# Splitting an accumulator's evacuation between ScalarE and VectorE, with the rounds of a fused convolution and MLP rearranged and its weights laid out in pairs

## The chip, the cores and the metric

One Trainium2 chip, one core. The metric is the device time of one execution in microseconds (us). A time is a median of several runs. A ratio is the mean time of one kernel's runs over that of the other kernel's runs of the same timing rounds (not the *rounds* of the kernel, which are explained below), so it is not quite the ratio of the medians quoted beside it. The interval is at 95%.

TensorE does the matmuls, into the memory called PSUM; ScalarE (ACT) and VectorE (DVE) read what it leaves there; GpSimd (POOL) works here on a buffer `E` in SBUF, the core's working memory; SyncE (SP), ACT and POOL start DMA transfers.

## The reference

```
w   = softmax(weight, over the 7 taps)            # 8 heads x 7
a   = causal depthwise conv of x[8, 4096, 192] with w (24 channels share a head)
h   = a.reshape(32768, 192) @ w_in                # 192 -> 2048
g   = where(h > 0, h, exp(min(h, 0)) - 1)         # ELU
out = g @ w_out                                   # 2048 -> 192, float32
```

## The kernel before

The tokens go through in 32 superblocks of 1024. Each superblock has 16 *up-projections*, one for each chunk of 128 of the 2048 features (six matmuls of 64x128 by 64x512 into one of three buffers of H in PSUM). ACT, POOL and DVE turn a buffer of H into `gT`. The *down-projection* is cut into *rounds* of two matmuls that add to `ops`, two PSUM banks, and are strewn between the up-projections. 64 rounds make one finished accumulator of 256 + 256 tokens; I call that stretch (8 up-projections, 64 rounds, one conv in two parts) a *half*. In the middle of each half stands one conv for a later superblock, which takes a turn of the three H buffers too.

How many rounds stand in which gap is set by tables:

```python
LAG = -3
GAPS = ((10,), (10,), (6,), (6,), (10,), (5, 6), (11,))
WCOLS = ((0, 256), (256, 640), (640, 1280), (1280, 2048))   # w_in is loaded in four pieces
EARLY_CONV = {3: (1, 0), 6: (1, 1), 9: (2, 0)}   # first convs, by up-projection
```

ELU of one tile, for each up-projection n and each u in (0, 1). `exp` is on ACT, the clamp on POOL, the rest on DVE:

```python
a.activation(E[:, n % NE, u, :], H[:, k, GS*u : GS*(u+1)], ACT.Exp)               # exp(h)
g.tensor_scalar(out=E[...], in0=E[...], 1.0, 0.0, op0=ALU.min, op1=ALU.max)       # min(exp(h), 1)
v.scalar_tensor_tensor(out=gT[...], in0=E[...], scalar=1.0, in1=H[...],
                       op0=ALU.subtract, op1=ALU.max)                              # max(E - 1, h)
```

An up-projection that takes a buffer of H waits until DVE is through with what was in it:

```python
def wait_slot(k):
    was = prior[k]
    ...
    if was[0] == "h":
        W(s_tt, 2 * was[1] + 2)
    else:
        conv_read(W, was[1])
```

With nine turns of three buffers in a half, the same places meet in every half. I number the up-projections behind the conv u1 to u8 (u8 is the last before the next conv). Then u4 takes the buffer of u1, u5 that of u2, and so on to u8, which takes u5's; the conv takes that of u6, u1 that of u7, and u2 that of u8; only u3 takes the conv's.

The finished accumulator is evacuated by ACT alone, in one copy of 2 x 384 columns, and the first round of the next half waits for it:

```python
def evac(key):
    W(s_swap, mm2_done[key])
    W(s_out[b], 32 * (n_half // 2))
    ...
    a.activation(osb[:, b].rearrange("p g k d -> p g (k d)"), ops[:, :, 0 : 2 * D], ACT.Copy).then_inc(s_oev)
```

## Time and profile before

| | before |
|---|---|
| time, median (range) | 747.87 us (747.39 to 748.05) |
| span of the profile | 746.5 us |
| busy: PE, DVE, ACT, POOL | 98, 85, 87, 89% |
| one half, in the steady part | 11.27 us |
| the part of it that is matmul work | 10.84 us |
| start of up-projection 25 | 49.12 us |

Two lines of the page of before: the busy time of each engine (us, share of the span, instructions), and the chain that ended last by engine.

```profile
PE 731.6 (98%) x11866; PEld 505.4 (68%) x11866; DVE 638.0 (85%) x1042; ACT 646.8 (87%) x1224; POOL 664.5 (89%) x1108
...
PE 93%; DVE 2%; POOL 2%; DMA 1%; ACT 1%; issue 0%
```

TensorE is the engine on the chain. A busy share of 98% says little about how well it is used, because overlapping matmuls count as busy: the 3072 of the up-projection take 378 ns each, 1161 us one after another, and their group is busy for 409.2 us. A better measure is the time from the start of one group of matmuls to the start of the next. Here is the timeline of before, TensorE's rows of one half with the rows of ACT and POOL that matter. Columns: start, duration (both us), engine, line, operation, written from read, shapes, how many merged, and in brackets how long the engine stood idle before and what ended it.

```profile
222.36 1.07 PE L770 MATMUL ops<-w_out,gT 64*128 64x192 f16 x22
...
223.27 1.46 PE L735 MATMUL H<-att,w_in 64*128 64x512 bf16 x12
223.54 0.82 ACT L474 ACTIVATE osb<-ops 128x768 f32<-128x768 f32 x1
...
224.23 3.10 ACT L515 ACTIVATE E<-H 128x512 f32<-128x512 f32 x6
...
224.56 0.99 PE L770 MATMUL ops<-w_out,gT 64*128 64x192 f16 x20
224.93 7.11 POOL L414 TENSOR_SCALAR E<-E 128x512 f32<-128x512 f32 x12 [0.47 <-ACT E L515]
...
225.39 0.81 PE L735 MATMUL H<-att,w_in 64*128 64x512 bf16 x6
...
226.03 0.99 PE L770 MATMUL ops<-w_out,gT 64*128 64x192 f16 x20
...
226.91 0.82 PE L735 MATMUL H<-att,w_in 64*128 64x512 bf16 x6
```

Six up-projection matmuls take 0.645 us (twelve take 224.56 - 223.27 = 1.29), a round takes about 0.0825 us (ten: 225.39 - 224.56 = 0.83), a part of the conv 0.20 us. So 8 x 0.645 + 64 x 0.0825 + 2 x 0.20 = 10.84 us is the work of a half. At 226.03 ten rounds take 0.88 us: the up-projection behind them is 0.05 us late. The 0.82 us copy on ACT stands in front of exponentials, and POOL is idle for 0.47 us before its run of clamps.

The same waits summed by who waited for whom (from 44 to 725 us of before; total us, times, longest):

```profile
POOL E L414 <- ACT E L515: 53.9, 159, 1.0
PEld ops L770 <- ACT osb L474: 11.2, 61, 0.2
PEld H L735 <- DVE gT L579: 8.5, 37, 0.4
```

PEld is the weight load. It runs ahead of the matmuls, so an idle weight loader is not yet an idle TensorE (one case in the timeline of after, below: 0.43 us of the one, 0.12 us of the other).

### The profile page before, as it was taken

What the parts mean: (1) busy time and instruction counts of PE and PEld (TensorE: products, weight loads), DVE (VectorE), ACT (ScalarE), POOL (GpSimd) and SP (SyncE); (2) the same over time, 40 slices, a digit from 0 to 9 for tenths busy, and PEclk for the clock granted to TensorE, in tenths of its full rate; (3) what the DMA queues carried; (4) which work ended last, traced back from release to release, by engine and by line L of the source; (5) the groups of instructions that cost most, each with busy time, mean ns of one, the idle gap of its engine ahead of it and who ended that gap; (6) DMA issues with size and microseconds to landing.
All of it is one profiled execution on the core that took longest, in us unless ns stands there. A gap on an engine that the chain in (4) does not pass through costs nothing.

```text
span 746.5 us, 28038 instructions
## 1 busy us (share of the span) xinstructions
PE 731.6 (98%) x11866; PEld 505.4 (68%) x11866; DVE 638.0 (85%) x1042; ACT 646.8 (87%) x1224; POOL 664.5 (89%) x1108
## 2 busy tenths in 40 slices
PE   6899999999999999999999999999999999999997
PEld 3466667666766676666766766766766766766666
DVE  5789889889889888898898898898898898888894
ACT  4888988988988988888989989989989989889883
POOL 8799999999899999899999899999999899898893
PEclk9999999999999999999999999999999999999999
DMA  9544435535435535345535345635345444244212
GB/s 168 93 76 91 62 70 93 94 61 92 63 68 94 93 60 95 57 74 95 82 71 94 46 84 94 77 77 70 64 91 94 67 87 81 53 89 81 46 44 66
DMA packets 132881, 58.93 MB, mean 79 GB/s; under 512 B 98068, under 2 KB 132372, under 8 KB 132756
## 3 DMA queue, kind: packets, MB, share of 16 engines
q0 software_dynamic: 44160, 17.28, 22.9%
q1 hardware_dynamic: 88308, 39.37, 21.9%
q8 instruction: 93, 1.52, 0.9%
q10 hardware_dynamic: 288, 0.49, 0.2%
q14 instruction: 32, 0.26, 0.1%
HBM read 35.61 MB, written 25.17 MB: 81 GB/s over the span
## 4 chain that ended last, share of the span: by engine, by line
PE 93%; DVE 2%; POOL 2%; DMA 1%; ACT 1%; issue 0%
PE H L735 45%; PE ops L770 44%; PE H L703 3%; DVE gT L579 2%; DMA xg<-in_x_dram 1%; ACT E L515 1%; POOL E L414 1%; PE H L770 1%; POOL w_in L369 1%; ACT csb L485 0%; POOL xg L364 0%; PE ops L703 0%; ACT osb L474 0%; PE ops L615 0%; POOL sel L384 0%
## 5 line engine op out<-in xcount | busy, mean ns | idle before, releaser
L579 DVE SCALAR_TENSOR_TENSOR gT<-E,H 128x512 f16<-128x512 f32 x1024 | 632.5, 681 | 90.9 <-POOL E L414 84.4
L414 POOL TENSOR_SCALAR E<-E 128x512 f32<-128x512 f32 x1024 | 603.9, 615 | 69.5 <-ACT E L515 62.1
L515 ACT ACTIVATE E<-H 128x512 f32<-128x512 f32 x1024 | 546.2, 608 | 73.5 <-PE H L735 64.8
L770 PE MATMUL ops<-w_out,gT 64*128 64x192 f16 x8064 | 426.4, 243 | 0.3
L770 PEld LDWEIGHTS ops<-w_out,gT 64*128 64x128 f16 x8064 | 346.9, 94 | 110.5 <-ACT osb L474 11.4
L735 PE MATMUL H<-att,w_in 64*128 64x512 bf16 x3072 | 409.2, 378 | 2.9 <-DVE gT L579 1.7
L735 PEld LDWEIGHTS H<-att,w_in 64*128 64x128 bf16 x3072 | 130.9, 94 | 111.7 <-DVE gT L579 12.8
L485 ACT ACTIVATE csb<-H 128x480 bf16<-128x480 f32 x118 | 60.9, 568 | 7.4 <-PE H L703 0.4
L474 ACT ACTIVATE osb<-ops 128x768 f32<-128x768 f32 x63 | 52.0, 826 | 6.2 <-PE ops L770 6.2
L364 POOL DMA_DIRECT2D xg<-in_x_dram x62 | 55.7, 899 | 0.1
L703 PE MATMUL H<-xg,Tm 64*128 64x240 bf16 x472 | 44.0, 263 | 0.1
L703 PEld LDWEIGHTS H<-xg,Tm 64*128 64x128 bf16 x472 | 21.2, 94 | 0.8 <-DVE gT L579 0.3
L485 ACT ACTIVATE csb<-ops 128x480 bf16<-128x480 f32 x6 | 3.5, 588 | 3.2 <-PE ops L703 3.2
L770 PE MATMUL H<-w_out,gT 64*128 64x192 f16 x128 | 5.9, 243 | 0.0
L703 PE MATMUL ops<-xg,Tm 64*128 64x240 bf16 x24 | 2.7, 306 | 3.3 <-DMA xg<-in_x_dram 3.1
L590 DVE COPY osb<-H 128x192 f32<-128x192 f32 x1 | 0.4, 358 | 6.3 <-PE H L770 6.3
L770 PEld LDWEIGHTS H<-w_out,gT 64*128 64x128 f16 x128 | 5.3, 94 | 0.0
L369 POOL DMA_DIRECT2D w_in<-in_moe_w_in_dram x7 | 4.6, 663 | 0.3 <-DMA wh<-in_weight_dram 0.3
L610 PE MATMUL ops<-zw 128*128 128x512 bf16 x9 | 3.6, 577 | 1.2 <-DVE zw L527 1.2
L615 PE MATMUL ops<-zw 64*128 64x512 bf16 x12 | 2.4, 381 | 2.3 <-ACT csb L485 2.3
L703 PEld LDWEIGHTS ops<-xg,Tm 64*128 64x128 bf16 x24 | 0.9, 97 | 5.2 <-issue 3.5
L615 PEld LDWEIGHTS ops<-zw 64*128 64x128 bf16 x12 | 0.6, 93 | 4.2 <-ACT csb L485 3.9
(49 smaller groups left out, 26.3 us busy)
## 6 DMA issues: line engine op xcount, KB each, us to landing
out_dram<-osb SPq DMA_DIRECT2D x126, 192.0 KB, 4.1
xg<-in_x_dram POOLq DMA_DIRECT2D x61, 240.0 KB, 5.6
w_out<-in_moe_w_out_dram POOLq DMA_DIRECT2D x1, 768.0 KB, 16.1
att<-csb SPq DMA_TRANSPOSE x31, 6.4
w_in<-in_moe_w_in_dram POOLq DMA_DIRECT2D x2, 240.0 KB, 9.0
xf<-in_x_dram ACTq DMA_DIRECT2D x1, 384.0 KB, 3.2
xf<-in_x_dram SPq DMA_DIRECT2D x1, 384.0 KB, 3.6
w_in<-in_moe_w_in_dram POOLq DMA_DIRECT2D x2, 144.0 KB, 4.2
```

Of the source, the lines that this page charges most:

```text
L364: g.dma_start(xg[:, b, v0 : v0 + whole, :], src).then_inc(s_x[b][part - 1], 16)
L369: g.dma_start(w_in[HP * r : HP * (r + 1), :, c0:c1], moe_w_in.rearrange("(p j) f -> p j f", j=3)[:, :, c0:c1],).then_inc(s_w[k], 16)
L414: g.tensor_scalar(out=E[:, n % NE, u, :], in0=E[:, n % NE, u, :], scalar1=1.0, scalar2=0.0, op0=ALU.min, op1=ALU.max,).then_inc(s_clp)
L474: a.activation(osb[:, b, :, :, :].rearrange("p g k d -> p g (k d)"), ops[:, :, 0 : 2 * D], ACT.Copy,).then_inc(s_oev)
L485: return a.activation(csb[:, s % 2, :].rearrange("p (j v h i) -> p h j v i", j=3, v=2 * WPG, h=HEADS)[:, h0 : h0 + HB], conv_bank(m)[:, b, ...
L515: a.activation(E[:, n % NE, u, :], H[:, k, GS * u : GS * (u + 1)], ACT.Exp).then_inc(s_exp)
L579: v.scalar_tensor_tensor(out=gT[:, s % NG3, q, u, :], in0=E[:, n % NE, u, :], scalar=1.0, in1=H[:, slot_of_pair[n] % 3, GS * u : GS * (u + ...
L610: pe.matmul(ops[:, 0, :], zw[:, 0:P], zw[:], start=True, stop=True)
L615: pe.matmul(ops[:, r, :], zw[HP * r : HP * (r + 1), 0:P], zw[HP * r : HP * (r + 1), :], start=True, stop=True, tile_position=(HP * r, 0),)
L703: ins = pe.matmul(to[:, b, n1 * hh : n1 * (hh + 1)], Tm[HP * rt : HP * (rt + 1), h, :], xg[HP * rt : HP * (rt + 1), s % NXB, :, :].rearran ...
L735: ins = pe.matmul(H[:, k % 3, GS * r : GS * (r + 1)], w_in[HP * r : HP * (r + 1), j, FC * q : FC * (q + 1)], att[HP * r : HP * (r + 1), s ...
L770: ins = pe.matmul(acc[:, g, d0 : d0 + D], gT[HP * rt : HP * (rt + 1), t % NG3, q, g, t0 : t0 + P], w_out[HP * rt : HP * (rt + 1), q, :], s ...
```

## The change

The intent is to relieve ACT: the copy is split, ACT takes bank 0 and DVE bank 1. The rounds are laid out anew (rounds 0, 1, 16, 7, 7, 7, 6, and 7 + 3 + 10 around the parts of the conv). The first convs come later. Features are paired: a partition takes two neighbouring rows of w_out, which makes runs of 1536 and not 768 bytes in that load, and w_in is read at stride 2 to match. The w_out load is also issued last.

```diff
-LAG = -3
-GAPS = ((10,), (10,), (6,), (6,), (10,), (5, 6), (11,))
-WCOLS = ((0, 256), (256, 640), (640, 1280), (1280, 2048))
+LAG = -5
+GAPS = ((), (1,), (16,), (7,), (7,), (7,), (6,), (7, 3, 10))
+WCOLS = ((0, 256), (256, 768), (768, 1280), (1280, 2048))
-EARLY_CONV = {3: (1, 0), 6: (1, 1), 9: (2, 0)}
+EARLY_CONV = {6: (1, 0), 8: (1, 1), 10: (2, 0)}
 ... (the order of the program follows GAPS)
             load_x(2, 1)
+            load_x(2, 2)
             g.dma_start(
-                w_out[:, :, :], moe_w_out.rearrange("(q p) d -> p q d", p=FC)
+                w_out.rearrange("p (q r) d -> p q (r d)", r=2), moe_w_out.rearrange("(q p r) d -> p q (r d)", p=FC, r=2)
             ).then_inc(s_w[4], 16)
-            load_x(2, 2)
 ... (ACT)
-                a.activation(
-                    osb[:, b, :, :, :].rearrange("p g k d -> p g (k d)"),
-                    ops[:, :, 0 : 2 * D],
-                    ACT.Copy,
-                ).then_inc(s_oev)
+                out_ready(W, key)
+                a.activation(*out_pieces(key, 0), ACT.Copy).then_inc(s_oev)
 ... (DVE now walks the program's order)
+            for item in order:
+                if item[0] == "o":
+                    for key in item[2]:
+                        out_ready(W, key)
+                        v.tensor_copy(*out_pieces(key, 1)).then_inc(s_od)
 ... (TensorE)
-                                w_in[HP * r : HP * (r + 1), j, FC * q : FC * (q + 1)],
+                                w_in[HP * r : HP * (r + 1), j,
+                                    2 * FC * (q // 2) + q % 2 : 2 * FC * (q // 2 + 1) : 2],
                                 W(s_oev, place[key])
+                                W(s_od, place[key])
```

More of the change, by code (lines that the diff above doesn't have):

```diff
@@ L24 @@
 BN = HB * CPH * 2 * WPG
-GAP_SPLIT = 4
 TAP = 6
@@ L32 @@
 NG3 = 2
-LAG = -3
-GAPS = ((10,), (10,), (6,), (6,), (10,), (5, 6), (11,))
-WCOLS = ((0, 256), (256, 640), (640, 1280), (1280, 2048))
-Q_PART = (0,) * 2 + (1,) * 3 + (2,) * 5 + (3,) * 6
+LAG = -5
+GAPS = ((), (1,), (16,), (7,), (7,), (7,), (6,), (7, 3, 10))
+WCOLS = ((0, 256), (256, 768), (768, 1280), (1280, 2048))
+Q_PART = (0,) * 2 + (1,) * 4 + (2,) * 4 + (3,) * 6
 WARM = (9, 1)
 CONV_AT = ((2, 1, 1), (10, 2, 0))
-EARLY_CONV = {3: (1, 0), 6: (1, 1), 9: (2, 0)}
+EARLY_CONV = {6: (1, 0), 8: (1, 1), 10: (2, 0)}
 FREE_CONV = 3
@@ L84, in bass_lightweight_conv__then__act_elu_kernel, with conv_at @@
     order = []
-    def conv_at(s, g, gap=None):
+    def conv_at(s, g, between=None):
         m = 2 * s + g - 2
@@ L90, in conv_at @@
         order.append(("c", m, 0))
-        between = []
-        if gap:
-            between, gap[:] = gap[:GAP_SPLIT], gap[GAP_SPLIT:]
         if between:
@@ L139, in bass_lightweight_conv__then__act_elu_kernel @@
         gaps = list(rounds_at.get(n, ()))
-        if len(gaps) == 2:
-            order.append(("o", gaps.pop(0)))
-        if n in EARLY_CONV:
-            conv_at(*EARLY_CONV[n])
-        if s:
-            for at, ahead, g in CONV_AT:
-                if at == i and s + ahead < NS:
-                    conv_at(s + ahead, g, gaps[0] if gaps else None)
-        if gaps and gaps[0]:
-            order.append(("o", gaps[0]))
+        convs = [EARLY_CONV[n]] if n in EARLY_CONV else []
+        convs += [
+            (s + ahead, g)
+            for at, ahead, g in CONV_AT
+            if at == i and s + ahead < NS and 2 * (s + ahead) + g - 2 >= FREE_CONV
+        ]
+        if convs and len(gaps) == 3:
+            order.append(("o", gaps[0]))
+            conv_at(*convs[0], gaps[1])
+            order.append(("o", gaps[2]))
+            continue
+        for conv in convs:
+            conv_at(*conv)
+        for gap in gaps:
+            order.append(("o", gap))
     last_slot = [take_slot(None) for _ in range(2)]
@@ L326, in out_group, with out_ready, out_pieces @@
             eng.dma_start(dst, osb[:, b, g, :, :]).then_inc(s_out[b], 16)
+        def out_ready(W, key):
+            t, half, kb = key
+            n_half = 2 * t + half
+            W(s_swap, mm2_done[key])
+            W(s_out[n_half % 2], 32 * (n_half // 2))
+        def out_pieces(key, g):
+            t, half, kb = key
+            b = (2 * t + half) % 2
+            if (t, half) == (last, 1):
+                return osb[:, b, g, kb, :], H[:, last_slot[kb] % 3, GS * g : GS * g + D]
+            return (
+                osb[:, b, g, :, :].rearrange("p k d -> p (k d)"),
+                ops[:, g, 0 : 2 * D],
+            )
         def turn_att(eng, s):
@@ L454, in evac @@
             def evac(key):
-                t, half, kb = key
-                n_half = 2 * t + half
-                W(s_swap, mm2_done[key])
-                b = n_half % 2
-                W(s_out[b], 32 * (n_half // 2))
-                if (t, half) == (last, 1):
-                    if kb == 0:
-                        a.activation(
-                            osb[:, b, :, 0, :],
-                            H[:, last_slot[0] % 3, :].rearrange("p (g t) -> p g t", g=2)[:, :, 0:D],
-                            ACT.Copy,
-                        ).then_inc(s_oev)
-                    else:
-                        a.activation(
-                            osb[:, b, 0, 1, :], H[:, last_slot[1] % 3, 0:D], ACT.Copy
-                        ).then_inc(s_oev)
-                        W(s_od, 1)
-                        out_group(a, t, half, 1, 1)
-                    return
-                a.activation(
-                    osb[:, b, :, :, :].rearrange("p g k d -> p g (k d)"),
-                    ops[:, :, 0 : 2 * D],
-                    ACT.Copy,
-                ).then_inc(s_oev)
+                out_ready(W, key)
+                a.activation(*out_pieces(key, 0), ACT.Copy).then_inc(s_oev)
+                if key == (last, 1, 1):
+                    W(s_od, place[key] + 1)
+                    out_group(a, last, 1, 1, 1)
             late = []
@@ L572, in _vector @@
             v.tensor_copy(Tm[:], Tr[:, :, ::-1]).then_inc(s_tm)
-            for n in range(NP):
-                s, q = divmod(n, NQ)
-                if s >= NG3:
-                    W(s_swap, mm2_done[s - NG3, 1, 0])
-                for u in range(2):
-                    W(s_clp, 2 * n + u + 1)
-                    v.scalar_tensor_tensor(
-                        out=gT[:, s % NG3, q, u, :],
-                        in0=E[:, n % NE, u, :],
-                        scalar=1.0,
-                        in1=H[:, slot_of_pair[n] % 3, GS * u : GS * (u + 1)],
-                        op0=ALU.subtract,
-                        op1=ALU.max,
-                    ).then_inc(s_tt)
-            b = (2 * NS - 1) % 2
-            W(s_swap, mm2_done[last, 1, 1])
-            W(s_out[b], 32 * (NS - 1))
-            v.tensor_copy(
-                osb[:, b, 1, 1, :], H[:, last_slot[1] % 3, GS : GS + D]
-            ).then_inc(s_od)
+            for item in order:
[3 more added lines that the diff above has]
+                        v.tensor_copy(*out_pieces(key, 1)).then_inc(s_od)
+                elif item[0] == "h":
+                    n = item[1]
+                    s, q = divmod(n, NQ)
+                    if s >= NG3:
+                        W(s_swap, mm2_done[s - NG3, 1, 0])
+                    for u in range(2):
+                        W(s_clp, 2 * n + u + 1)
+                        v.scalar_tensor_tensor(
+                            out=gT[:, s % NG3, q, u, :],
+                            in0=E[:, n % NE, u, :],
+                            scalar=1.0,
+                            in1=H[:, slot_of_pair[n] % 3, GS * u : GS * (u + 1)],
+                            op0=ALU.subtract,
+                            op1=ALU.max,
+                        ).then_inc(s_tt)
         @block.tensor
@@ L736, in _tensor @@
                                 H[:, k % 3, GS * r : GS * (r + 1)],
-                                w_in[HP * r : HP * (r + 1), j, FC * q : FC * (q + 1)],
+                                w_in[
+                                    HP * r : HP * (r + 1),
+                                    j,
+                                    2 * FC * (q // 2) + q % 2 : 2 * FC * (q // 2 + 1) : 2,
+                                ],
                                 att[HP * r : HP * (r + 1), s % 2, j, 0:GS],
@@ L814, in _sync @@
                         t, half, kb = key
-                        W(s_oev, place[key] + 1)
-                        if (t, half) != (last, 1):
-                            for g in range(2):
+                        for g in range(2):
+                            W((s_oev, s_od)[g], place[key] + 1)
+                            if (t, half) != (last, 1):
                                 out_group(sy, t, half, g)
-                        elif kb == 0:
-                            for g in range(2):
-                                out_group(sy, t, half, g, 0)
-                        else:
-                            out_group(sy, t, half, 0, 1)
+                            elif (g, kb) != (1, 1):
+                                out_group(sy, t, half, g, kb)
             for b in range(2):
```

## The prediction

> **What bounds it now.** TensorE. The page gives PE 98% busy, and the chain of waits that ended last is 93% PE, nearly all of it the two matmul groups (up-projection into H 45%, down-projection into ops 44%). Reading start-to-start times in the timeline, six up-projection matmuls take 0.645 us, a down-projection round of two takes 0.0825 us, and half a conv takes 0.20 us. A half-superblock (8 up-projections, 64 rounds, two conv halves) therefore needs 5.16 + 5.28 + 0.40 = 10.84 us. From 44 to 725 us it really takes about 11.21 us, so only 0.37 us of each half (22 us in all) is not matmul work. Most of this, about 18 us, is TensorE waiting before an up-projection for one of the three H buffers to be freed by DVE; about 3 us is the hand-over inside the conv. The evacuation of ops (0.83 us on ACT, 63 times) is not a direct wait: two up-projections (1.29 us) hide it. It delays the next exponentials, though: POOL then idles 0.47 us per half (in the timeline, waiting for ACT) and runs its clamps back to back (0.59 us each), so the next H buffers come free late. ACT, POOL and DVE are 87, 89 and 85% busy.
>
> **What the change does.**
> - ACT's 768-column copy becomes 384 on ACT and 384 on DVE in parallel. My estimates from the 0.83 us (768 columns) and 0.36 us (192 on DVE): about 0.43 us on ACT, 0.5 us on DVE. ACT loses 25 us in all, DVE gains about 30 us and goes to 89-90%.
> - Rounds are rearranged with the same counts: a long gap of 16 after three near-adjacent up-projections, then even gaps of 6-7, and 20 around the conv. Total TensorE work is unchanged. Walking one half with the trace's latency (2.8 us from the end of an up-projection to DVE freeing its buffer) I get waits of 0.1-0.2 us before the second up-projection after the conv, almost none in the even gaps, and one more bank hand-over at the conv (0.05 us). Estimate: 11.09 us per half instead of 11.21, about 7 us over 61 halves.
> - Early convs move from pairs 3, 6, 9 to 6, 8, 10. This removes the 3.05 us wait for the conv input (landing at 18.2 us), but pairs from 10 on then meet the last w_in copy (issued 20.1, 6.3 us to land). Net about 2 us.
> - w_out's load has half as many pieces, twice as long[...]; w_out is not waited for in this trace, so I count nothing.
> - w_in weights are read at stride 2 bf16.[...] Each load shows 94 ns[...].
>
> **Predicted:** 739 us, range 730 to 747. Faster by over 2%: 0.18; within 2%: 0.79; slower by over 2%: 0.03.
>
> **What would show it.** Right: ACT's osb copies near 0.43 us with DVE copies near 0.5 us; up-projection weight loads still 94 ns; the wait of up-projections for DVE halves; POOL's idle before the clamps falls; period per half near 11.1 us; the first down-projection starts some 3 us earlier; no wait on the conv input at 15-18 us.
>
> **What would make it wrong.** DVE's copy sits in order in front of gate work: if it delays freeing buffers, or the round after two up-projections waits for DVE's copy, the gain vanishes (745-750).[...] If the waits vanish altogether and the start gains over 4 us, it is near 728.

The sum: 747.87 us of before, less about 7 for the steady part and about 2 for the start, is 739.

## The result, and the profile after

| | before | after |
|---|---|---|
| time, median (range) | 747.87 us (747.39 to 748.05) | 743.3 us (742.13 to 744.1) |
| ratio to before | | 0.9939 (0.9921 to 0.9956) |
| span of the profile | 746.5 us | 741.6 us |
| one half, from up-projection 57 to 489 (54 halves) | 11.27 us | 11.20 us |
| start of up-projection 25 | 49.12 us | 47.92 us |

Of the 4.9 us between the two spans, 1.2 us are there at up-projection 25; another 3.9 us come by up-projection 489, evenly but for 0.4 us that before loses once between 201 and 217; the rest of the program gives 0.2 us back. The 1.2 us are one profile against one, and that of after starts late: its first up-projection begins at 12.53 us and that of before at 10.76 (why, is told under the table of the runs). Counted from there, 38.36 us to up-projection 25 became 35.39.

The page of after, the same two lines:

```profile
PE 730.1 (98%) x11866; PEld 502.6 (68%) x11866; DVE 657.3 (89%) x1106; ACT 636.4 (86%) x1224; POOL 663.7 (89%) x1108
...
PE 94%; DMA 3%; POOL 1%; ACT 0%; DVE 0%; issue 0%
```

ACT went from 646.8 to 636.4 us and DVE from 638.0 to 657.3. The groups of after that do the evacuation, and the weight loads of the up-projection (busy us, mean ns of one, idle us before):

```profile
L733 PEld LDWEIGHTS H<-att,w_in 64*128 64x128 bf16 x3072 | 131.9, 94 | 105.2 <-DVE gT L583 30.6 <-DMA w_in<-w_in 1.6 <-ACT att L468 0.8
...
L473 ACT ACTIVATE osb<-ops 128x384 f32<-128x384 f32 x63 | 31.3, 497 | 9.5 <-PE ops L773 9.5
L575 DVE COPY osb<-ops 128x384 f32<-128x384 f32 x63 | 34.6, 549 | 4.6 <-PE ops L773 4.6
```

The weight loads take 94 ns as before, at stride 2 (131.9 us in 3072 loads; before has 130.9). For 384 columns ACT's copy takes 497 ns and DVE's 549; in before ACT's copy of 768 columns took 826 ns, and DVE's one copy, of 192, took 358.

One half in the timeline of after:

```profile
229.55 0.38 PE L701 MATMUL H<-xg,Tm 64*128 64x240 bf16 x4
...
230.29 1.00 PE L773 MATMUL ops<-w_out,gT 64*128 64x192 f16 x20
...
231.13 1.57 PE L733 MATMUL H<-att,w_in 64*128 64x512 bf16 x12
231.37 0.50 ACT L473 ACTIVATE osb<-ops 128x384 f32<-128x384 f32 x1
231.74 0.55 DVE L575 COPY osb<-ops 128x384 f32<-128x384 f32 x1
231.87 0.33 PEld L733 LDWEIGHTS H<-att,w_in 64*128 64x128 bf16 x6 [0.43 <-DVE gT L583]
231.98 3.04 ACT L513 ACTIVATE E<-H 128x512 f32<-128x512 f32 x6
...
232.67 9.58 POOL L431 TENSOR_SCALAR E<-E 128x512 f32<-128x512 f32 x16 [0.80 <-ACT E L513]
...
233.27 1.48 PE L773 MATMUL ops<-w_out,gT 64*128 64x192 f16 x32
...
234.65 0.82 PE L733 MATMUL H<-att,w_in 64*128 64x512 bf16 x6
```

Both copies end (at 231.87 and 232.29 us) before the first round of the next half wants the banks. But u2 is held up: its weight loads stand still for 0.43 us until DVE has freed the buffer of u8. Of that, TensorE loses 0.12 us: u1, u2 and nothing else should take 1.29 us, and the next rounds come 232.54 - 231.13 = 1.41 us after. Behind the gap of 16 rounds u4 comes 0.06 us late (16 x 0.0825 = 1.32, and 234.65 - 233.27 = 1.38).

The waits of after, from 44 to 720 us:

```profile
POOL E L431 <- ACT E L513: 50.9, 61, 1.6
...
PEld H L733 <- DVE gT L583: 25.8, 60, 0.4
PEld ops L773 <- issue: 12.3, 60, 0.3
```

The wait for ACT's copy (11.2 us of weight-loader idle before) is no longer named; idle time of the same size stands at the same place as "issue" (12.3 us), and in neither kernel does TensorE lose anything there. The wait of the up-projections' weight loads for DVE tripled, from 8.5 to 25.8 us, although the kernel is faster. This view counts the weight loader's idle time. From start-to-start times, the loss of TensorE before up-projections fell:

| mean loss per half (us), 100 to 640 us | before | after |
|---|---|---|
| before u1 (behind the conv) | 0.13 | 0.01 |
| before u2 | 0 | 0.11 |
| before u4 (in after behind the long gap) | 0 | 0.065 |
| before the other up-projections | 0.17 | 0.01 |
| around and inside the conv (hand-over of `ops` between sides) | 0.07 | 0.13 |

(These are what is left of each start-to-start time when the work named above is taken off; they leave out hundredths that stand everywhere, so that u2's 0.11 is 0.125 with the one behind it. In before, "the other" are 0.064 before u5, 0.086 before u6 and 0.021 before u7, and nothing before u8.)

At the start, the chain of before held the wait for the first conv's input; the chain of after holds the last load of w_in and its copy to the other partitions. The lines of the waits between 12 and 44 us, first before:

```profile
PE ops L703 <- DMA xg<-in_x_dram: 3.1, 1, 3.1
```

and after:

```profile
PE H L733 <- DMA w_in<-w_in: 1.1, 1, 1.1
```

### The profile page after: what moved, and what is told of

Same layout as the page of the kernel before. It is cut to its first block, busy times and chain, and to the rows that moved or that the text cites. A ratio compares the mean times of both kernels' runs of the same rounds, so it can differ in the third digit from the quotient of the medians.

```text
span 741.6 us, 28196 instructions
## 1 busy us (share of the span) xinstructions
PE 730.1 (98%) x11866; PEld 502.6 (68%) x11866; DVE 657.3 (89%) x1106; ACT 636.4 (86%) x1224; POOL 663.7 (89%) x1108
## 3 DMA queue, kind: packets, MB, share of 16 engines
q0 software_dynamic: 43136, 17.28, 24.1%
## 4 chain that ended last, share of the span: by engine, by line
PE 94%; DMA 3%; POOL 1%; ACT 0%; DVE 0%; issue 0%
PE ops L773 45%; PE H L733 45%; PE H L701 3%; DMA w_in<-in_moe_w_in_dram 1%; DMA w_in<-w_in 1%; PE H L773 1%; POOL E L431 1%; POOL w_in L386 1%; POOL xg L381 0%; DVE gT L583 0%; ACT E L513 0%; DMA wh<-in_weight_dram 0%; ACT csb L483 0%; DVE osb L575 0%
## 5 line engine op out<-in xcount | busy, mean ns | idle before, releaser
L583 DVE SCALAR_TENSOR_TENSOR gT<-E,H 128x512 f16<-128x512 f32 x1024 | 622.1, 681 | 68.4 <-POOL E L431 68.1
L733 PEld LDWEIGHTS H<-att,w_in 64*128 64x128 bf16 x3072 | 131.9, 94 | 105.2 <-DVE gT L583 30.6
L473 ACT ACTIVATE osb<-ops 128x384 f32<-128x384 f32 x63 | 31.3, 497 | 9.5 <-PE ops L773 9.5
L575 DVE COPY osb<-ops 128x384 f32<-128x384 f32 x63 | 34.6, 549 | 4.6 <-PE ops L773 4.6
L701 PEld LDWEIGHTS H<-xg,Tm 64*128 64x128 bf16 x472 | 18.0, 93 | 3.7 <-issue 1.2
```

Of the source, the lines that this page charges most:

```text
L473: a.activation(*out_pieces(key, 0), ACT.Copy).then_inc(s_oev)
L575: v.tensor_copy(*out_pieces(key, 1)).then_inc(s_od)
L583: v.scalar_tensor_tensor(out=gT[:, s % NG3, q, u, :], in0=E[:, n % NE, u, :], scalar=1.0, in1=H[:, slot_of_pair[n] % 3, GS * u : GS * (u + ...
L701: ins = pe.matmul(to[:, b, n1 * hh : n1 * (hh + 1)], Tm[HP * rt : HP * (rt + 1), h, :], xg[HP * rt : HP * (rt + 1), s % NXB, :, :].rearran ...
L733: ins = pe.matmul(H[:, k % 3, GS * r : GS * (r + 1)], w_in[HP * r : HP * (r + 1), j, 2 * FC * (q // 2) + q % 2 : 2 * FC * (q // 2 + 1) : 2 ...
```

## The experiments

Theory: the split pays only with the new rounds, since it decides where DVE's copy stands in DVE's queue; what is left in the steady part is the reuse of an H buffer, about 2.9 us from the end of the up-projection that filled it to the start of the one that takes it; the start is bound by a chain of loads. Rivals: the split pays by relieving ACT; POOL's throughput is the limit; strided weights cost something hidden; hand-overs on TensorE are the floor.

The twelve runs, with after in front:

| run | time, us | ratio to before | interval | one half, us | up-projection 25 at, us |
|---|---|---|---|---|---|
| after | 743.30 | 0.9939 | 0.9921 to 0.9956 | 11.20 | 47.92 |
| c_split | 813.62 | 1.0867 | 1.0851 to 1.0884 | 12.34 | 51.20 |
| c_rounds | 751.08 | 1.0037 | 1.0024 to 1.0049 | 11.31 | 48.80 |
| c_early | 747.57 | 0.9987 | 0.9974 to 1.0000 | 11.27 | 47.90 |
| c_pair | 746.97 | 0.9978 | 0.9966 to 0.9991 | 11.27 | 47.55 |
| d_lateconv | 743.42 | 0.9940 | 0.9928 to 0.9953 | 11.20 | 47.75 |
| d_swapload | 741.81 | 0.9925 | 0.9912 to 0.9937 | 11.20 | 47.76 |
| d_r18 | 745.28 | 0.9965 | 0.9952 to 0.9979 | 11.23 | 46.65 |
| d_noclamp | 742.80 | 0.9930 | 0.9918 to 0.9943 | 11.19 | 47.63 |
| e_r18nc | 743.90 | 0.9940 | 0.9928 to 0.9953 | 11.21 | 47.94 |
| e_turn | 740.81 | 0.9900 | 0.9887 to 0.9914 | 11.17 | 47.57 |
| e_order | 747.00 | 0.9982 | 0.9969 to 0.9996 | 11.27 | 47.73 |
| e_best | 741.37 | 0.9912 | 0.9896 to 0.9928 | 11.19 | 49.35 |

The last two columns come from one profile each. The start varies from run to run: the first up-projection of these profiles begins between 10.8 and 14.1 us, although nothing in front of it differs in most of these kernels. In the late ones 24 early matmuls, the same in every kernel, take 310 ns each and not 221 or 222. A trace lists the granted clock in stretches. The list begins at 4.26 us in before and at 10.63 us in after, and right there the pace of like matmuls of after goes from 0.21 to 0.11 us a pair. (The view of windows gives 1.00 for time in front of the list, which hides this.) The list begins between 3.9 and 5.9 us in seven of the fourteen profiles, and between 9.8 and 12.9 us in the others: after, d_swapload, d_noclamp and the four e runs. These seven are the late ones.

Six profiles, of before, c_split, c_rounds, c_early, c_pair and d_lateconv, also list a clock of 0.50 for 3.4 us (c_split 6.8) of the start; the record's mean clock is 0.995 to 0.998 for these six and 0.999 or 1.000 for the other eight. In before this is from 17.91 to 21.33 us. It begins while TensorE waits for the conv's input, and the twelve up-projection matmuls at 19.35 us take 2.44 us, against 1.46 later. Whether the wait brings the slow stretch, no run here shows. In the timed runs the mean granted clock goes with the time: c_early took 745.88 us at 1.000, 747.24 and 747.57 at 0.998, 748.09 and 748.12 at 0.995. Some of what looks like a gain at the start can be this. That is why I read the steady part from the period of a half, and the start from the timed runs as well as the profile.

### c_split: the split alone

```diff
 GAPS = ((10,), (10,), (6,), (6,), (10,), (5, 6), (11,))    # as before
+                a.activation(*out_pieces(key, 0), ACT.Copy).then_inc(s_oev)
+                        v.tensor_copy(*out_pieces(key, 1)).then_inc(s_od)
```

> The kernel before with only the evacuation split between ACT and DVE; rounds, early convs and weight layout as before. Main theory: the split pays only with the new order of rounds, because in the old order the accumulation ends after the first up-projection behind the conv, so DVE's copy stands in its queue behind that pair's two gate operations, which finish about 2.8 us after the up-projection, while the next rounds are due 1.3 us after the accumulation ends. TensorE should then wait 0.8 to 1.2 us per half for DVE's copy: 780 to 820 us. Rival (the split by itself is what gains, by relieving ACT): 741 to 745 us.

Measured: 813.62 us, 8.7% slower than before. The waits (44 to 720 us), and one half of its timeline:

```profile
PE ops L768 <- DVE osb L574: 59.1, 55, 1.1
```

```profile
241.46 1.46 PE L732 MATMUL H<-att,w_in 64*128 64x512 bf16 x12
241.73 0.50 ACT L472 ACTIVATE osb<-ops 128x384 f32<-128x384 f32 x1
242.09 1.29 DVE L582 SCALAR_TENSOR_TENSOR gT<-E,H 128x512 f16<-128x512 f32 x2 [0.89 <-POOL E L430]
...
243.30 0.55 DVE L574 COPY osb<-ops 128x384 f32<-128x384 f32 x1
...
244.00 1.00 PE L768 MATMUL ops<-w_out,gT 64*128 64x192 f16 x20 [1.07 <-DVE osb L574]
```

TensorE is through with two up-projections at 241.46 + 1.29 = 242.75 us and wants to go on with rounds. DVE's copy has to wait for the two gate operations of u1 in its queue (242.09 to 243.38), although the accumulator had been finished at 241.46. It ends at 243.85, and TensorE goes on at 244.00. So TensorE loses 244.00 - 242.75 = 1.25 us here; the view's mean of 59.1 / 55 = 1.07 us counts only from the modelled end of the last matmul. A half took 12.34 - 11.27 = 1.07 us longer: the waits before u5, u6 and u7, together 0.17 us in the kernel before, are gone in c_split. ACT's copy had long been done. The rival is out: the split by itself does not pay. What ACT's relief would be worth without the wait for DVE's copy, this run cannot tell.

### c_rounds: the new rounds alone

```diff
-GAPS = ((10,), (10,), (6,), (6,), (10,), (5, 6), (11,))
+GAPS = ((), (1,), (16,), (7,), (7,), (7,), (6,), (7, 3, 10))
```

(with LAG = -5 and the program's order for it; one copy of 768 columns on ACT)

> The kernel before with only the new rounds; one copy of 768 columns on ACT. Main theory: ACT's longer copy stands in front of the exponential of the first up-projection behind the conv and delays the run of 16 clamps by 0.2 to 0.3 us per half, about half of which TensorE sees: 747 to 754 us, no better than before. Rival (the rounds by themselves gain, by evening out the H waits): 741 to 745 us.

Measured: 751.08 us, 0.4% slower than before; a half takes 11.31 us. From its timeline:

```profile
233.58 1.57 PE L736 MATMUL H<-att,w_in 64*128 64x512 bf16 x12
233.82 0.82 ACT L475 ACTIVATE osb<-ops 128x768 f32<-128x768 f32 x1
...
234.52 3.06 ACT L516 ACTIVATE E<-H 128x512 f32<-128x512 f32 x6
...
235.23 9.57 POOL L415 TENSOR_SCALAR E<-E 128x512 f32<-128x512 f32 x16 [0.90 <-ACT E L516]
...
237.21 0.82 PE L736 MATMUL H<-att,w_in 64*128 64x512 bf16 x6
```

u1 ends at 233.58 + 0.645 = 234.23 us and ACT begins its exponential 0.29 us later; in after the same is 231.98 - 231.78 = 0.20 us. u4 may start 2.98 us after u1's end, in after 2.87. So both the split and the new rounds cost time alone, and together they gain. With the new rounds in place the split is worth 11.31 - 11.20 = 0.11 us a half, about 6 us in all, because it takes 0.33 us from ACT in front of u1.

### c_early, c_pair, d_lateconv, e_order, d_swapload: the start

c_early is before with `EARLY_CONV = {6: (1, 0), 8: (1, 1), 10: (2, 0)}` only:

> The kernel before with only the early convs moved to pairs 6, 8 and 10. Theory: the wait for the conv input goes, but pair 10 still meets the copy of w_in, so the start gains 1 to 2 us and the steady part stays: 746 to 747 us. Rival (the start is bound by the DMA and nothing comes of it): 747.9 us.

c_pair is before with the paired weights only (w_out in 1536-byte runs, w_in at stride 2, other WCOLS, the w_out load last):

> The kernel before with only the paired features: w_out in 1536-byte runs, w_in read at stride 2, w_in cut at other columns, w_out loaded last. Theory: no effect on the steady part (weight loads stay at 94 ns) and none at the start: 747.9 us within 0.7 us. Rival (strided weight loads cost something that the other parts hide): above 749 us, and weight loads over 94 ns.

Both leave the half at 11.27 us. c_early gains 0.0013 and c_pair 0.0022, each all at the start. The interval of c_early reaches 1.0000 and its median lies just outside the range expected, so its gain is barely clear of the noise. For c_pair I had expected nothing. Its weight loads show no cost of the stride:

```profile
L735 PEld LDWEIGHTS H<-att,w_in 64*128 64x128 bf16 x3072 | 131.5, 94 | 110.9 <-DVE gT L579 12.7 <-issue 5.7 <-ACT att L451 0.8
```

(131.5 us in 3072 loads; before has 130.9.) Its gain is the conv's input: it lands 9.55 us after its issue, at 16.9 us, against 10.89 us and 18.2 us in before. e_order is before with the w_out load merely issued behind the third conv input:

> The kernel before with only the w_out load issued last, after the third conv input. If this is what made the paired layout 1.5 us faster at the start: conv input landing near 16.9 us, ratio 0.997 to 0.999. If it is the halved number of w_out pieces: landing near 18.2 us, ratio 0.9995 to 1.0005.

Its ratio is 0.9982, and the input lands 9.90 us after its issue; TensorE waits 1.2 us for it, and 3.1 in before. Here the load had been issued 0.64 us later than in before, for reasons upstream, so the landing time itself (17.8 us) is between the two that I named. Most of the shorter wait is TensorE's own late start in this profile (its first up-projection begins 1.7 us later than in before). The timed runs, 0.9982 against c_pair's 0.9978, speak for the order of the loads, and not the length of w_out's runs, as most of c_pair's gain. Part of it goes with the clock: three of e_order's five runs had a granted clock of 0.999 or more, and one of before's nine; at 0.997 and 0.998 e_order is 0.7 us ahead (two runs against seven). The time from issue to landing decides nothing. With the w_out load third in line behind the input it is 10.2 to 11.1 us (before, c_split, c_rounds, c_early). With it fourth it is 8.9 to 10.3 us in eight profiles (seven of them with paired weights too), where after (10.28) and d_lateconv (8.85) have the very same loads.

I had also asked after the number of w_out's pieces (the queue of that load takes 44160 packets in before and 43136 in after); no run here shows a gain from halving it: with it c_pair has 0.9978, without it e_order 0.9982, and the intervals overlap. Whether, and why, a load issued *after* the conv's input delays that input is left open.

d_lateconv is after with the early convs back at 3, 6 and 9:

> The kernel after with the early convs put back to pairs 3, 6 and 9. Theory: the gain of the early convs (0.0013 of the time alone) and that of the paired layout (0.0022 alone, all of it at the start, where the conv input then lands at 16.9 us and not 18.2) are the same 1 to 1.5 us, because both end at the last copy of w_in, so nothing is lost without the first: 742.5 to 744 us, a ratio to before of 0.992 to 0.995. Rival (they add up): 744.3 to 745.5 us, 0.9952 to 0.997.

It takes 743.42 us, ratio 0.9940, as after. The two gains of the start do not add up: with the convs of after (at 6, 8 and 10) the start hangs on the last copy of w_in, with those of this run (at 3, 6 and 9) on the conv's input (landing at 16.8 us here, TensorE waiting 1.7 us for it), and both bring up-projection 25 to about the same place (47.92 and 47.75 us, though the profile of after had the later start). d_swapload moves that one:

```diff
-            load_x(1, 2)
             load_w_in(3, (0,))
+            load_x(1, 2)
```

> The kernel after with the last part of w_in loaded ahead of the second conv input. Theory: the start of the kernel after is bound by that load and its copy to the other partitions (landing at 26.2 us, TensorE idle for 1.1 us before pair 10); ahead by one 240 KB transfer it should land near 24.5 us: 1 us faster than after, ratio to before 0.9915 to 0.9935. Rival (the start is bound by the clamps, the copy is met by chance): ratio 0.994 as after.

741.81 us, ratio 0.9925: the wait for the copy of w_in has gone from the profile and 1.5 us (741.81 against 743.3) from the median, in different timing rounds and with intervals that overlap. All five runs had a granted clock of 0.999 or more, and among runs at 1.000 the means are only 0.7 us apart. The direction is as expected; its size is not settled.

### d_r18, d_noclamp, e_r18nc: what is left of the waits

d_r18 is after with

```diff
-GAPS = ((), (1,), (16,), (7,), (7,), (7,), (6,), (7, 3, 10))
+GAPS = ((), (1,), (18,), (7,), (6,), (7,), (5,), (7, 3, 10))
```

> The kernel after with two rounds moved into the long gap: 1, 18, 7, 6, 7, 5, 7+3+10. Theory: what is left in the steady part is the reuse of H buffers after about 2.87 us: the second up-projection after the conv waits 0.12 us, the third after the long gap 0.07 us. Two more rounds there (0.165 us) take the second wait away and leave the first, so 0.03 to 0.07 us per half: 1 to 4 us faster than after, ratio to before 0.989 to 0.9925. Rival (POOL's clamps set the pace, and gaps of 5 rounds between them run into it): same or slower than after, ratio 0.994 to 0.998.

("The third after the long gap" means the up-projection behind that gap, u4.) A miss: 745.28 us, slower than after; a half takes 11.23 us. The wait before u4 is gone, that before u2 stayed, and a new one of 0.09 us appeared before u8, behind the gap of five:

```profile
235.16 0.81 PE L733 MATMUL H<-att,w_in 64*128 64x512 bf16 x6
...
238.19 0.59 PE L773 MATMUL ops<-w_out,gT 64*128 64x192 f16 x10
238.68 0.82 PE L733 MATMUL H<-att,w_in 64*128 64x512 bf16 x6
```

I had named POOL's pace as the rival for this. Two runs decide against it. d_noclamp cuts one of a half's 16 clamps to a single column. Its result is wrong, though the comparison with the reference passed:

```diff
+                    m = 1 if u and n % 8 == 7 else GS
                     g.tensor_scalar(
-                        out=E[:, n % NE, u, :],
-                        in0=E[:, n % NE, u, :],
+                        out=E[:, n % NE, u, 0:m],
+                        in0=E[:, n % NE, u, 0:m],
```

> Wrong on purpose: the kernel after with one of each half's 16 clamps cut to one column, which takes about 0.5 us from POOL per half. Theory: POOL is fed just in time by the up-projections, so the latency of the chain and not POOL's throughput is what TensorE waits for; what the second up-projection no longer waits, the one after the long gap waits instead: 0 to 1.5 us faster than after, ratio to before 0.992 to 0.994. Rival (POOL's back-to-back run is the limit): 4 to 11 us faster than after, ratio below 0.989.

742.80 us, ratio 0.9930, a half 11.19 us: POOL's relief is worth 0.01 us a half. POOL now simply waits more for ACT (in after 50.9 us, 61 times), while the up-projections wait for DVE exactly as in after (25.8 us, 60 times):

```profile
POOL E L432 <- ACT E L514: 78.3, 122, 1.6
...
PEld H L734 <- DVE gT L584: 25.8, 60, 0.4
```

e_r18nc does both edits:

> Wrong on purpose: both edits at once, rounds 1, 18, 7, 6, 7, 5, 7+3+10 and one of each half's 16 clamps cut to one column. Theory: two limits stand side by side in the kernel after, the latency of H reuse and POOL's pace. Each edit alone moved nothing because the other limit stayed (0.9965 and 0.9930 against 0.9939 for after); both together should gain 0.06 to 0.12 us per half, 4 to 7 us: ratio to before 0.984 to 0.989. Rival (TensorE's own work with its hand-overs is the floor, nothing is left to gain): 0.992 to 0.996.

Another miss: 743.90 us, ratio 0.9940, a half 11.21 us, and the wait before u8 is still there (0.086 us):

```profile
236.12 0.81 PE L734 MATMUL H<-att,w_in 64*128 64x512 bf16 x6
...
239.64 0.82 PE L734 MATMUL H<-att,w_in 64*128 64x512 bf16 x6
```

This shows what the limit is. u8 takes the buffer of u5. In d_r18, u5 ends at 235.16 + 0.645 = 235.81 and u8 starts at 238.68, 2.87 us later; in e_r18nc 239.64 - (236.12 + 0.645) = 2.87; in after u1 to u4 is 2.87. With POOL loaded or relieved it is the same number, and the clamp that was cut is u5's own: it ends 2.08 us after u5 in d_r18 and 1.65 us after it in e_r18nc, and both times the second gate operation ends at 2.82. So it is the latency of the chain ACT, POOL, DVE for two tiles that sets the time here, and not POOL's pace. Between u5 and u8 stand two up-projections and, in d_r18, 6 + 7 + 5 = 18 rounds, 2 x 0.645 + 18 x 0.0825 = 2.78 us of work: 0.09 us too little, which is the wait seen. So the count of rounds between two up-projections that share a buffer must be at least (2.87 - 1.29) / 0.0825 = 19 here. With 7 + 7 + 6 = 20 there after has just enough, and I took two away.

This count holds where the chain finds its engines free, as behind u1 and u5. It is not the same for every buffer. In after u2 and u3 follow close on u1, and their last gate operations end 3.27 and 3.72 us after them (u1: 2.83), so u6, which takes u3's buffer, needs about (3.72 + 0.06 - 1.29) / 0.0825 = 30 rounds in between (0.06 us is what lies between the last gate operation and the start of u4 behind u1). And u8's first gate operation begins 0.086 us after its clamp ended, not 0.034 as for u1, because DVE is still at the gates of u7: from u1 to u8 it runs them without a break, one in 0.60 us. So, as an estimate from these numbers, about 0.05 us of the wait before u2 is a queue on DVE. No run relieved DVE, so its throughput is a rival left untested for that wait.

### e_turn: one hand-over less

Each round has one of two sides (which half of the partitions feeds which bank). Where the side changes, the kernel lets TensorE wait (for `s_swap`) until the former run of rounds has landed. With one change more in the conv, hand-overs take 0.13 us of a half in after against 0.07 in before. In after the side alternates from gap to gap, so it changes twice inside the conv. Here the counts stay and the sides are chosen so that it changes there once:

```diff
+SIDES = (1, 0, 1, 1, 1, 0, 0, 0, 1)
...
-            at, turned = [0, 0], 0
+            at, sides = [0, 0], iter(SIDES)
...
                 for size in sizes:
+                    turned = next(sides)
...
-                    turned ^= 1
```

> The kernel after with the same round counts, but with the sides of the rounds (which half of the partitions feeds which bank) chosen so that they change once and not twice inside the conv. Theory: the hand-over in the first half of the conv (0.04 us) goes, but the second up-projection after the conv waits that much longer, since its H buffer comes free a fixed time after the last up-projection before the conv: within 1 us of after, ratio 0.992 to 0.9955. Rival (hand-overs are TensorE time like any other): 2.5 us faster than after, ratio 0.989 to 0.992.

The rival won: 740.81 us (four runs), ratio 0.9900, a half 11.17 us. One half from its timeline, u1 and u2, one round, u3, the long gap and u4:

```profile
241.76 1.65 PE L734 MATMUL H<-att,w_in 64*128 64x512 bf16 x12
243.24 0.25 PE L774 MATMUL ops<-w_out,gT 64*128 64x192 f16 x2
...
243.97 1.49 PE L774 MATMUL ops<-w_out,gT 64*128 64x192 f16 x32
245.29 0.82 PE L734 MATMUL H<-att,w_in 64*128 64x512 bf16 x6
```

Here u2 loses 243.24 - 241.76 - 1.29 = 0.19 us, and u4 nothing (245.29 - 243.97 = 1.32). In the means, the mechanism that I named did work, the wait before u2 grew from 0.125 to 0.17 us. But the wait before u4 fell from 0.065 to 0.02 by the same amount. I had overlooked that u4 is timed from the end of u1, and u1 itself now comes 0.04 us earlier. From u1 to u4 the 2.87 us of latency set the time. From u4 round to the next u1 TensorE does nothing but work and hand-overs, and there every hundredth counts in full. This also explains d_r18: its two rounds left the stretch that counts (0.165 us) but made the other longer and opened the wait before u8.

### e_best: a candidate

After with the load order of d_swapload and `GAPS = ((), (1,), (17,), (7,), (6,), (7,), (6,), (7, 3, 10))`:

> A candidate that should beat both: the kernel after with the last w_in load ahead of the second conv input, and one round moved into the long gap (1, 17, 7, 6, 7, 6, 7+3+10), which takes the 0.07 us wait there without making POOL's clamps bunch as with 18. Expected 1 us from the start and 0 to 2 us from the steady part: ratio to before 0.9895 to 0.9925.

741.37 us, ratio 0.9912, a half 11.19 us. It beats before, and after by its median; its profiled run was the slowest of five, with a late start. The wait before u4 is gone, but most of it is back before u6 (0.049 us, 0.010 in after), the buffer that needs about 30 rounds: the 17 + 7 + 6 here are 30, and in after the wait before u4 had helped. e_turn is better in the steady part. Both beat before with intervals clear of 1, and e_turn's interval lies clear of that of after. No run combines the two, so what they give jointly is not known.

## Why the prediction was right or wrong

The prediction was 739 us, within 2%; measured are 743.3 us, within 2% and within the range. The range, 730 to 747, reached from a gain of 2.4% to almost none, so that the time fell in it says little. The gain predicted, 9 us, was twice the gain measured.

- *TensorE bounds it, with little to win.* Right. Of the 11.27 us of a half (I had put 11.21), 0.43 are not matmul work, and after has 0.36.
- *The copies.* I estimated 0.43 us on ACT and 0.5 us on DVE; measured are 0.50 and 0.55. I had scaled ACT's by columns, but half the columns took 0.497 us of 0.826 and not 0.413: as an estimate from these two, 2 x 0.497 - 0.826 = 0.17 us does not go with the columns.
- *The steady part: "11.09 us per half instead of 11.21, about 7 us".* The mis-sized term. The halves went from 11.27 to 11.20, a gain of 0.07 and not 0.12 us. The wait before u2, which I put at 0.1 to 0.2, is 0.12, and the even gaps have none, both right. What I left out of the sum is the wait of 0.065 us before u4, behind the long gap. It is about the whole difference between the two gains (the rest of the 0.11 us between 11.09 and 11.20 was in my starting figure), and it is the one that sets the time, as e_turn shows: whatever lies between u1 and u4 fills up to 2.87 us.
- *"One more bank hand-over at the conv (0.05 us)."* Right: 0.07 became 0.13.
- *The start: "Net about 2 us".* Measured 1.2 us in the profiles, 3.0 counted from the first up-projection; the clock at the start (above) blurs both. Right in kind: the wait for the conv's input went and that for w_in's copy came. I counted nothing for the order of the loads, which by its ratio alone is worth as much (e_order) and does not add up with it (d_lateconv).
- *"Up-projection weight loads still 94 ns", at stride 2.* Right: 94 ns.
- *"The wait of up-projections for DVE halves."* Wrong as a reading of the waits view, where it tripled (8.5 to 25.8 us), since that view counts the weight loader's idle. In TensorE's own losses it fell from 0.30 to about 0.2 us a half.
- *"POOL's idle before the clamps falls."* Wrong for the stretch behind the copy, where it rose from 0.47 to 0.80 us; in total it fell only from 53.9 to 50.9 us. In c_rounds it is 0.90, so of the two parts it is the split that lowers it, by 0.10.
- *"The first down-projection starts some 3 us earlier."* 30.22 against 32.46 us: 2.2, with a late start in the profile of after.
- *DVE's copy in front of gate work as the danger.* It did not strike in after, and c_split shows why: with the old rounds a half is 1.07 us longer, 66 us in all. The new rounds are what makes the split possible.

So the change is two parts that each lose alone (8.7% and 0.4%) and together gain about 4 us in the steady part, and two parts that each gain 1 to 1.6 us at the start (the first of them barely clear of the noise) and gain that only once.

## What to carry to other kernels

When work moves to another engine's queue, ask first what stands in front of it there at the moment it falls due; the schedule has to put its due time where that queue is short (in c_split it was not: a half took 1.07 us longer). When buffers are reused after a fixed chain of engines, count the work between the use and the reuse of each one, and look in the trace how long the chain takes for each, since a queue on one engine can make it longer (about 0.05 us of the wait before u2, by the estimate above). Here only the stretches where the count fell short waited: work taken out of those gained nothing (the hand-over between u8 and u2 in e_turn: the wait before u2 grew by 0.045 us), and work taken out of the others counted in full (the same hand-over, from u4 to the next u1: a half went from 11.20 to 11.17 us). The gains at the start, a chain of loads, did not add up: each uncovered the next load. And before two starts are compared, look at where the trace's list of granted clock begins (4.26 us in before, 10.63 in after).
